# Local attention in front of two dense layers: 12 attention units of two 128-query blocks instead of 16 of two 96-query blocks

## The chip, the cores and the metric

The kernel runs on one core of a Trainium2 chip. The metric is the device time of one execution in microseconds (us); lower is better. Engines are named as in the profile: PE (matmuls), PEld (PE's weight loads), DVE (VectorE), ACT (ScalarE), POOL (GpSimd), and SP, whose queue issues most of the DMAs. Every engine works through its own queue in order.

## The reference

```python
# q, k, v: (4, 8, 768, 64); mem_k, mem_v: (4, 8, 8, 64); chunk, left, right = 32, 16, 8
for c in range(24):                                  # 24 chunks of 32 queries
    q_c = q[:, :, 32*c : 32*c + 32]
    lo, hi = max(0, 32*c - 16), min(768, 32*c + 40)
    k_full = concatenate([mem_k, k[:, :, lo:hi]], axis=2)      # up to 64 keys
    v_full = concatenate([mem_v, v[:, :, lo:hi]], axis=2)
    s = (q_c @ k_full.T) / 8
    a = exp(s - max(s)); a = a / (sum(a) + 1e-9)
    out[:, :, 32*c : 32*c + 32] = a @ v_full
x = out as (3072, 512)
h = (x @ w1) * (x @ w2) @ w3;  x = h @ w_out         # 512 -> 1024 -> 512
y = (x @ w_a) * (x @ w_b) @ w_out2                   # 512 -> 1536 -> 512
```

All data are float32.

## The kernel before

The 3072 tokens are cut into six tiles of 512. A first stretch makes the product of `w3` and `w_out` on PE (tiles `wps`, 32 fp32 matmuls for each of two halves, every one of them two records in the trace). Its weights come as 64-bit words: ACT scales them in two passes (`w_scale`), and DVE joins them in two instructions (`w_bits`). Then, for four of the tiles, come the first dense layer's products (`psA`, `psB`, 12 matmuls each, then `psY`). Last come the seven-product forms of the other tiles and of the second layer (lines 1047 and 1346), which the change does not touch.

Attention is woven into the first stretch and into the four tiles. It goes in units `u`. A unit is two blocks of `GQ` = 96 queries of all 8 heads, 192 tokens, so there are 16 units; the first three lie in the `wps` stretch. Its steps, by their functions:

- `a_k`, `a_q`, `a_v` load raw keys (`kraw`), queries (`q`) and values (`v`) through SP. `a_keys` copies the keys into windows `kw`, on DVE or ACT.
- `a_scores` makes scores `sc`: small matmuls of 64 rows by 32 columns, for 8 head pairs, `NC` = 3 chunks and 2 row halves. A chunk's scores go to 32 partitions of their own, so 2 x 3 places of the PE array are in use. With two records each these are 96 records.
- `a_max` (mask, row maximum, two subtractions into `tt`, on DVE), `a_exp` (two exponentials on ACT) and `a_norm` (sum, reciprocal, two multiplications on DVE) are the softmax.
- `a_trans` transposes `tt` on PE into `pt` (8 transposes); `a_pt` copies that to `p2` on ACT. `a_pv` multiplies it with `v` into `xp`: matmuls of 64 rows by 64 columns in 2 x 2 places, 96 records. `a_x` takes `xp` out as a high part (ACT) and a low part (DVE) `xt`, which `psA` and `psB` read.

Where each step stands in the program is a table. Slot `BASE[u] + s` holds a step; `attn_slot` writes the next slot's steps at fixed places of the `wps` loops (from place `g` = 9 of the first half on, two places to a `k`), and later `between` does so after each `psA` or `psB` (12 matmuls). Buffers are single for `kw`, `q`, `v`, `p2`; there are two `tt`, used in turn.

Of the kernel before, what the change touches and what calls it, by code (L numbers as in the profile page):

```python
# [17 lines left out]
GQ = 96  # L18
NG = S // GQ
KW = 128  # L20
# [27 lines left out]
def tile_attention_moe(  # L48
# [54 lines left out]
    tt = [att.tile([GQ, NH * KR + 1], F32, tag="t", bufs=2, name="tt") for _ in range(2)]  # L103
# [14 lines left out]
    def a_k(u):  # L118
        if u >= NA:
            return  # L120
        k = ks[u] = att.tile([P, NE, 4 * KW], F32, tag="kraw", bufs=1, name="kraw")
# [3 lines left out]
        src = bass.AP(src.tensor, src.offset, [[row[0], P], [step, NE], x])  # L125
        nc.sync.dma_start(out=k, in_=src)

# [26 lines left out]
    def a_keys(u):  # L154
        if u >= NA:
            return
        k = ks.pop(u).rearrange("p e (h k) -> p (e h) k", h=4)
        p, a, e = k.ap
        win = bass.AP(
            k.tensor, k.offset + NMEM * e[0], [p, a, [CHUNK * e[0], NC], [e[0], KEYS - NMEM]]  # L160
        )
        if u in (1, 2):
            nc.scalar.activation(kw[:, :, :, NMEM:], win, AF.Copy)
        else:
            nc.vector.tensor_copy(kw[:, :, :, NMEM:], win)
        if new_batch(u):
            nc.vector.tensor_copy(
                kw[:, :, :, 0:NMEM], k[:, :, None, 0:NMEM].to_broadcast([P, NH, NC, NMEM])
            )

# [20 lines left out]
    def with_eps(u):  # L191
        t = tt[u % 2]
        p, x = t.ap
        return bass.AP(t.tensor, t.offset, [p, [KR * x[0], NH], [(KEYS + 1) * x[0], 2], [x[0], KEYS + 1]])
# [3 lines left out]
    def a_max(u):  # L198
        sc = scs.pop(u)
        for e in range(NE):  # L200
            g = (NE * u + e) % NG
            hs = slice(4 * e, 4 * e + 4)
            if g == 0:
                a_edge(sc, slice(0, CHUNK), hs, NMEM, NMEM + LEFT)
            if g == NG - 1:
                a_edge(sc, slice(GQ - CHUNK, GQ), hs, KEYS - RIGHT, KEYS)
        t = tt[u % 2][:, : NH * KR].rearrange("p (a x) -> p a x", x=KR)[:, :, 1:]
        t = t.rearrange("p a (r k) -> p a r k", r=2)
        mx = att.tile([GQ, 2, NH], F32, tag="mx", bufs=2, name="mx")
# [12 lines left out]
        soft[u] = (sc, t, mx, sm)  # L222
# [87 lines left out]
    for u in range(NA):  # L310
# [22 lines left out]
    at(0, (lambda u: w_load(), 0, False), (a_v, 0, False))  # L333
    NEED = []
    for i in range(NT1):
        u = -(-TT * (i + 1) // (NE * GQ)) - 1
        NEED.append(BASE[u] + (13 if u > 2 else 10))
# [323 lines left out]
    for i in range(2):  # L661
# [14 lines left out]
    whole = []  # L676
# [31 lines left out]
    for half in range(2):  # L708
        banks = [psd.tile([P, 512], F32, tag="d", name="wps") for _ in range(4)]
        for k in range(8):  # L710
            for m in range(4):
# [6 lines left out]
                if half == 0:  # L718
                    if g == 9:
                        amid[:] = [w_turn, w_next]  # L720
                    if g >= 9:
                        attn_slot()
                    if g in (0, 2, 4, 6, 8):
                        w_tick(g < 8)
                    if g == 0:
                        a_k(0)
                        a_q(0)
                    if g == 7:
                        a_keys(0)
                        a_k(1)  # L730
                    if g == 9:
                        bound[0] = len(wsrc)
                    if g == 13:
                        w_turn()
                else:
                    attn_slot()
                    for i in range(2 * len(S3)):
                        if (2, 6, 3, 7, 7, 8, 11, 12)[i] == g:
# [3 lines left out]
                    if g == 9:  # L742
                        split_hi(wsm[0][:, 0, :], whole[0])
                        split_lo(wsm[0][:, 1, :], whole[0], wsm[0][:, 0, :])
                    if g in (1, 4, 5, 6, 9, 10, 13, 14):
                        w_tick()
# [87 lines left out]
    PACE = 6  # L834

    def between():
# [9 lines left out]
        if not converting:  # L846
            for _ in range(1 + (n % PACE == 0)):
# [831 lines left out]
```

## Time and profile before

| | before |
|---|---|
| median of 3 runs | 1030.5 us (1030.47 to 1031.82) |
| the profiled execution's own time | 1030.02 us |
| its span (first to last instruction) | 1028.2 us |
| mean granted TensorE clock | 0.999 |
| PE busy | 1019.4 us (99%) |
| DVE, ACT, POOL busy | 729.0, 493.7, 160.0 us |

The span is what the trace covers; the execution's own time is 1.8 us longer. A busy PE means that some matmul was under way. Matmuls overlap, so a group's summed time and its mean say less than the starts of the groups in the timeline.

### The profile page before, as it was taken

The numbers are of one execution on the slowest core, as the hardware profiler recorded it, in microseconds if no ns is written. First come the engines' busy times: TensorE is split into PE (matmuls) and PEld (weight loads), VectorE is DVE, ScalarE is ACT, GpSimd is POOL, SyncE is SP. The second block draws the span as 40 slices with busy tenths as digits, with TensorE's granted clock in tenths as the row PEclk, the third lists the DMA queues.
The fourth block names the chain that finished last, engine by engine and source line by source line (L and its number), as shares of the span: only waits on it lengthen the run. The fifth ranks groups of instructions, "written<-read, shape, count | busy, mean of one in ns | idle before, by whom it ended". The sixth has DMA issues, their size and how long they took to land.

```text
span 1028.2 us, 18741 instructions
## 1 busy us (share of the span) xinstructions
PE 1019.4 (99%) x7294; PEld 817.0 (79%) x7294; DVE 729.0 (71%) x1158; ACT 493.7 (48%) x886; POOL 160.0 (16%) x210
## 2 busy tenths in 40 slices
PE   9999999999999999999999999999999999999997
PEld 3468888888888888888888888888888888888886
DVE  4879936666565365768777778976677896666695
ACT  5676613444443345565645345643433663344352
POOL 0011397132231100001011101002100000101000
PEclk9999999999999999999999999999999999999999
DMA  8986557778886534496657774987545697324166
GB/s 326 324 225 206 156 200 246 237 231 272 258 296 199 159 115 159 138 317 191 199 188 227 234 251 139 343 235 195 130 156 176 216 310 180 101 87 134 37 205 122
DMA packets 150297, 208.76 MB, mean 203 GB/s; under 512 B 60481, under 2 KB 107457, under 8 KB 148929
## 3 DMA queue, kind: packets, MB, share of 16 engines
q1 hardware_dynamic: 132112, 163.22, 49.5%
q0 software_dynamic: 11008, 42.47, 13.7%
q10 hardware_dynamic: 7088, 1.88, 1.0%
q8 instruction: 57, 0.93, 0.4%
q14 instruction: 32, 0.25, 0.1%
HBM read 157.20 MB, written 52.43 MB: 204 GB/s over the span
## 4 chain that ended last, share of the span: by engine, by line
PE 52%; DVE 1%; issue 0%
PE ps L1047 34%; PE ops L1346 17%; PE psY L97 2%; DVE tmp L1063 0%; DVE g L1073 0%; DVE w L110 0%; DVE ob L1383 0%; DVE tmp L1382 0%; DVE cs L613 0%
## 5 line engine op out<-in xcount | busy, mean ns | idle before, releaser
L1047 PE MATMUL ps<-x,w 128*128 128x512 f32 x1848 | 422.9, 389 | 0.3 <-DVE tmp L1063 0.2
L1047 PEld LDWEIGHTS ps<-x,w 128*128 128x128 f32 x1848 | 346.5, 188 | 73.5 <-DVE tmp L1063 1.4
L1059 ACT ACTIVATE tmp<-ps 128x512 f32<-128x512 f32 x132 | 78.8, 597 | 245.7 <-PE ps L1047 175.8
L1346 PE MATMUL ops<-wo,fo 128*128 128x512 f32 x756 | 174.6, 389 | 0.0
L1346 PEld LDWEIGHTS ops<-wo,fo 128*128 128x128 f32 x756 | 141.8, 188 | 29.9 <-ACT x L1401 0.6
L97 PE MATMUL psY<-g,wo 128*128 128x512 f32 x576 | 134.5, 391 | 0.0
L110 DVE TENSOR_TENSOR w<-w 128x512 fp32r<-128x512 f32 (+1 forms) x176 | 105.5, 619 | 37.7 <-ACT w L107 37.7
L97 PEld LDWEIGHTS psY<-g,wo 128*128 128x128 f32 x576 | 107.4, 188 | 22.4
L1296 DVE TENSOR_TENSOR tmp<-ps,tmp 128x512 f32<-128x512 f32 x108 | 74.3, 688 | 31.9 <-PE ps L1047 27.0
L97 PE MATMUL psA<-xt,w 128*128 128x512 f32 x384 | 94.3, 394 | 0.0
L97 PE MATMUL psB<-xt,w 128*128 128x512 f32 x384 | 93.8, 393 | 0.0
L107 ACT ACTIVATE w<-w 128x512 fp32r<-128x512 f32 (+1 forms) x176 | 92.5, 572 | 0.0
L97 PEld LDWEIGHTS psB<-xt,w 128*128 128x128 f32 x384 | 71.2, 188 | 15.0
L97 PEld LDWEIGHTS psA<-xt,w 128*128 128x128 f32 x384 | 70.9, 188 | 14.9
L1236 DVE TENSOR_TENSOR wo<-gl,wo 128x512 fp32r<-128x512 f32 x90 | 59.6, 685 | 31.6 <-ACT wo L107 31.6
L941 POOL DMA_DIRECT2D w<-wc x36 | 19.4, 540 | 306.9 <-PE ps L1047 275.7
L419 ACT ACTIVATE raw<-raw 128x512 f32<-128x512 f32 (+1 forms) x62 | 46.1, 744 | 32.7 <-DMA raw<-in_wab 18.7
L107 ACT ACTIVATE wo<-gl 128x512 fp32r<-128x512 f32 x90 | 52.9, 625 | 9.3 <-PE ops L1346 8.9
L97 PE MATMUL wps<-w_f 128*128 128x512 f32 x112 | 50.0, 598 | 0.6 <-DVE w_f L425 0.6
L420 ACT ACTIVATE raw<-raw 128x512 uint32<-128x512 uint32 (+1 forms) x62 | 46.1, 744 | 0.0
L780 DVE TENSOR_TENSOR gv<-psB,gv 128x512 f32<-128x512 f32 x32 | 22.0, 686 | 27.1 <-PE psB L97 25.2
L97 PEld LDWEIGHTS wps<-w_f 128*128 128x128 f32 x112 | 20.7, 190 | 25.3 <-issue 21.9
(106 smaller groups left out, 1012.3 us busy)
## 6 DMA issues: line engine op xcount, KB each, us to landing
fo<-fo SPq DMA_DIRECT2D x42, 768.0 KB
w<-wc POOLq DMA_DIRECT2D x36, 512.0 KB, 3.8
w<-wc POOLq DMA_DIRECT2D x36, 384.0 KB, 3.4
raw<-in_wab SPq DMA_DIRECT2D x24, 512.0 KB
v<-in_vw SPq DMA_DIRECT2D x64, 168.0 KB
kraw<-in_kt SPq DMA_DIRECT2D x16, 512.0 KB
raw<-in_w3a SPq DMA_DIRECT2D x6, 1024.0 KB
q<-in_qt SPq DMA_DIRECT2D x16, 384.0 KB
```

Source lines behind the costliest of these rows:

```text
L97: nc.tensor.matmul(o, lhsT=l, rhs=r, start=first, stop=last)
L107: nc.scalar.activation(hi, src, AF.Copy)
L110: nc.vector.tensor_tensor(lo, src, hi.bitcast(F32), ALU.subtract)
L419: nc.scalar.activation(h, h, AF.Prelu, scale=2.0**-112, alpha=2.0**32)
L420: nc.scalar.activation(l, l, AF.Copy, scale=2.0**-29)
L780: nc.vector.tensor_tensor(gv, psB[:, :TT], gv, ALU.mult)
L941: nc.gpsimd.dma_start(out=t[:, 1, :c].bitcast(F32), in_=wseq[n][:, :c])
L1047: nc.tensor.matmul(ps, lhsT=w[i][:, a, k, :], rhs=xs[i][:, b, k, :], start=first and n == 0, stop=n == 5, skip_group_check=not first,)
L1059: nc.scalar.activation(z, ps, AF.Copy)
L1236: low.tensor_tensor(e[:, 1, :n], src, e[:, 0, :n].bitcast(F32), ALU.subtract)
L1296: nc.vector.tensor_tensor(z, ps, y, ALU.add)
L1346: nc.tensor.matmul(ps[s], lhsT=w[:, b, P * s : P * s + P], rhs=e[:, a, :], start=fresh and j == 0 and n == 0, stop=j == HF - 1 and n == 2, ...
```

## The change

A unit is now two blocks of 128 queries, 256 tokens, so there are 12 units, two of them in the `wps` stretch. `NC` is 4: scores use 2 x 4 places of the PE array and 128 partitions. There is one `tt` instead of two. From unit 2 on the raw keys come one block at a time through one buffer `khalf`, and each block's copy into `kw` stands in a slot of its own; a unit then has two key loads and two copies. The first load of attention data comes later, the slots are new, and so are the places where weights are converted in the `wps` stretch. Three of the four first-half results now go out as plain copies (`whole`) and are split into high and low parts later. The weight sums of the later layers (`cw_step`, `d_weights`) start after step 18.

```diff
-GQ = 96
+GQ = 128
-KW = 128
+KW = 160
-    tt = [att.tile([GQ, NH * KR + 1], F32, tag="t", bufs=2, name="tt") for _ in range(2)]
+    tt = [att.tile([GQ, NH * KR + 1], F32, tag="t", bufs=1, name="tt")]
-    def a_k(u):
+    def a_k(u, es=(0, 1)):
...
+        if len(es) == 2:
+            k = p0.tile([P, NE, 4 * KW], F32, tag="kraw", bufs=1, name="kraw")
+            src = bass.AP(src.tensor, src.offset, [[row[0], P], [step, NE], x])
+        else:
+            k = att.tile([P, 1, 4 * KW], F32, tag="khalf", bufs=1, name="khalf")
+            src = bass.AP(src.tensor, src.offset + step * es[0], [[row[0], P], [step, 1], x])
         nc.sync.dma_start(out=k, in_=src)
-    def a_keys(u):
+    def a_keys(u, es=(0, 1)):
...
+        for e in es:
...
+            w = kw[:, 4 * e : 4 * e + 4]
+            if u in (0, 1, 2):
+                nc.scalar.activation(w[:, :, :, NMEM:], win, AF.Copy)
+            else:
+                nc.vector.tensor_copy(w[:, :, :, NMEM:], win)
-    BASE = [0, 6, 13, 23, 29, 36]
-    NX = len(BASE)
-    BASE += [BASE[-1] + 7 * i for i in range(1, NA - NX + 1)]
-    SLOTS = {0: (6, 7, 9, 10), 1: (6, 7, 10, 11), 2: (6, 7, 8, 8)}
+    BASE = [5, 12]
+    BASE += [25, 33, 41, 48, 56, 64, 71, 79, 86, 94]
+    SLOTS = {0: (6, 8, 8, 10), 1: (6, 6, 9, 9)}
-        if u > 0:
-            at(BASE[u] - 3, (a_keys, u, True))
-            at(BASE[u] - 2, (a_k, u + 1, True))
+        if u == 1:
+            at(BASE[0] + 0, (a_k, 1, False))
+            at(BASE[1] - 3, (a_keys, 1, True))
+        if u > 1:
+            at(BASE[u] - 7, (a_half(a_k, 0), u, False))
+            at(BASE[u] - 6, (a_half(a_keys, 0), u, True))
+            at(BASE[u] - 6, (a_half(a_k, 1), u, True))
+            at(BASE[u] - 3, (a_half(a_keys, 1), u, True))
-        if half == 0 and m == 0:
-            whole.append(stage.tile([P, 4, CH // 2], F32, tag="cs", bufs=2, name="whole").rearrange("p i c -> p (i c)")[:, :CH])
-            nc.scalar.activation(whole[0], banks[m], AF.Copy)
+        if half == 0 and m < 3:
+            if m % 2 == 0:
+                keep[:] = [stage.tile([P, 4, CH // 2], F32, tag="cs", bufs=2, name="whole").rearrange("p i c -> p (i c)")]
+            whole.append(keep[0][:, CH * (m % 2) : CH * (m % 2) + CH])
+            nc.scalar.activation(whole[m], banks[m], AF.Copy)
             return
-        if not converting:
-            for _ in range(1 + (n % PACE == 0)):
+        if not converting and n > 18:
+            for _ in range(1 + (n % 6 == 0)):
```

What the program's order becomes shows at three places. First PE, from the program's start, before: `wps` is the product of `w3` and `w_out`, `sc`, `pt` and `xp` are a unit's scores, transposes and values; the count behind an x is of matmuls.

```order
L97 MATMUL wps<-w_f 128x512 x20
L97 MATMUL sc<-kw,q 32x64 x48
L97 MATMUL wps<-w_f 128x512 x12
L249 MATMUL pt<-id_sb,tt 128x96 x8
L97 MATMUL sc<-kw,q 32x64 x48
L97 MATMUL wps<-w_f 128x512 x6
L97 MATMUL xp<-p_400,v 64x32 x48
```

And PE at the same place now:

```order
L97 MATMUL wps<-w_f 128x512 x30
L97 MATMUL sc<-kw,q 32x64 x64
L97 MATMUL wps<-w_f 128x512 x12
L260 MATMUL pt<-id_sb,tt 128x128 x8
L97 MATMUL wps<-w_f 128x512 x2
L97 MATMUL sc<-kw,q 32x64 x64
L97 MATMUL wps<-w_f 128x512 x2
L97 MATMUL xp<-p_476,v 64x32 x64
```

Unit 0's scores moved from behind the 20th `wps` matmul to behind the 30th, two before the end of the first half (32 matmuls), and a unit has 64 small matmuls where it had 48.

Second ACT, around the end of the first `wps` half, before (`raw` are weights being scaled, `whole` and `wo` take the first half's four results out of PE's banks):

```order
L419 ACTIVATE raw_208<-raw_208 128x1024
L420 ACTIVATE raw_208<-raw_208 128x1024
L227 ACTIVATE tt<-tt 96x4x128 x2
L163 ACTIVATE kw<-kraw 128x24x56
L682 ACTIVATE whole<-wps 128x512
L684 ACTIVATE wo<-wps 128x512 x3
L255 ACTIVATE p_400<-pt 128x768
```

ACT at the same place now:

```order
L434 ACTIVATE raw_208<-raw_208 128x1024
L435 ACTIVATE raw_208<-raw_208 128x1024
L434 ACTIVATE raw_217<-raw_217 128x1024
L435 ACTIVATE raw_217<-raw_217 128x1024
L699 ACTIVATE whole<-wps 128x512
L238 ACTIVATE tt<-tt 128x4x128 x2
L699 ACTIVATE whole<-wps 128x512 x2
L701 ACTIVATE wo<-wps 128x512
```

One more weight block is scaled ahead of the first result, and unit 0's two exponentials now stand between the first result's copy and the second's.

Third DVE in the tiles, now, around one unit's softmax: `kw<-khalf` is the copy of one block of the next unit's keys, and `gv<-psB` takes PE's `psB` results.

```order
L200 TENSOR_TENSOR sc<-sc,mask_sb 32x2x4x16
L222 TENSOR_REDUCE mx<-sc 128x16
L227 TENSOR_TENSOR tt<-sc,mx 128x2x4x64 x2
L793 TENSOR_TENSOR gv<-psB,gv 128x512
L246 TENSOR_REDUCE sm<-tt 128x16
L247 RECIPROCAL sm<-sm 128x16
L249 TENSOR_TENSOR tt<-tt,sm 128x4x128
L173 COPY kw<-khalf 128x16x56
L796 TENSOR_TENSOR g_2126<-gv,g_2126 128x512
L249 TENSOR_TENSOR tt<-tt,sm 128x4x128
L793 TENSOR_TENSOR gv<-psB,gv 128x512
```

The copy of a block's keys moved into the middle of the unit before, one slot behind the load that it needs, and a `gv<-psB` stands behind it on DVE.

## Rows read from the trace of the kernel before

**Rows 1.** The page, part 1: busy us, share of the span, instructions.
```profile
PE 1019.4 (99%) x7294; PEld 817.0 (79%) x7294; DVE 729.0 (71%) x1158; ACT 493.7 (48%) x886; POOL 160.0 (16%) x210
```

**Rows 2.** Busy us by stretch, with granted clock, DMA share and GB/s.
```profile
core 0: us, PE busy (x) PEld busy (x) DVE busy (x) ACT busy (x) POOL busy (x), PEclk, DMA share, GB/s
26.00:76.00 50.00, 48.64 (x698) 27.27 (x697) 39.27 (x55) 36.28 (x51) 5.12 (x4) 1.00 0.87 275
30.00:35.00 5.00, 5.00 (x13) 2.24 (x12) 4.80 (x7) 3.41 (x4) 0.00 (x0) 1.00 1.03 401
...
76.00:360.00 284.00, 284.00 (x3635) 233.08 (x3634) 182.11 (x269) 127.46 (x219) 100.85 (x106) 1.00 0.70 224
```

**Rows 3.** PE's waits over the span: total us, times, longest us.
```profile
PE wps L97 <- DVE w_f L425: 0.6, 2, 0.3
PE pt L249 <- issue: 0.6, 1, 0.6
...
PE sc L97 <- DVE kw L167: 0.2, 1, 0.2
```

**Rows 4.** PE's timeline, one unit's period in the tiles: start us, us.
```profile
237.71 1.19 PE L97 MATMUL sc<-kw,q 64*32 64x64 f32 x96
238.84 3.02 PE L97 MATMUL psB<-xt,w 128*128 128x512 f32 x12
241.69 0.82 PE L249 MATMUL pt<-id_sb,tt 96*128 96x96 f32 x8
...
247.95 1.60 PE L97 MATMUL xp<-p,v 64*64 64x32 f32 x96
...
252.34 2.88 PE L97 MATMUL psB<-xt,w 128*128 128x512 f32 x12
255.06 2.88 PE L97 MATMUL psA<-xt,w 128*128 128x512 f32 x12
257.87 1.19 PE L97 MATMUL sc<-kw,q 64*32 64x64 f32 x96
```

**Rows 5.** PE's groups by form: busy us, mean ns of one.
```profile
L97 PE MATMUL xp<-p,v 64*64 64x32 f32 x1536 | 25.7, 220 | 0.0
L97 PE MATMUL sc<-kw,q 64*32 64x64 f32 x1536 | 19.1, 219 | 0.2 <-DVE kw L167 0.2
L249 PE MATMUL pt<-id_sb,tt 96*128 96x96 f32 x128 | 13.5, 247 | 0.6 <-issue 0.6
```

**Rows 6.** PE's timeline at the start of the first stretch.
```profile
9.23 17.33 PE L97 MATMUL wps<-w_f 128*128 128x512 f32 x40
```

**Rows 7.** Timeline of the first stretch: a weight block, unit 0's softmax, the results.
```profile
25.78 0.33 SPq L404 DMA_DIRECT2D raw<-in_w3b  x1
...
30.65 0.29 DVE L189 TENSOR_TENSOR sc<-sc,mask_sb 32x128 f32<-32x128 f32 x1
...
30.97 1.22 DVE L211 TENSOR_REDUCE mx<-sc 96x16 f32<-96x1024 f32 x1
...
33.40 1.17 ACT L419 ACTIVATE raw<-raw 128x1024 f32<-128x1024 f32 x1 [1.59 <-DMA raw<-in_w3b]
...
34.06 1.28 DVE L216 TENSOR_TENSOR tt<-sc,mx 96x512 f32<-96x512 f32 x2
...
34.46 1.13 ACT L420 ACTIVATE raw<-raw 128x1024 uint32<-128x1024 uint32 x1
...
35.48 1.15 ACT L227 ACTIVATE tt<-tt 96x512 f32<-96x512 f32 x2
...
38.21 1.56 ACT L684 ACTIVATE wo<-wps 128x512 fp32r<-128x512 f32 x3
```

**Rows 8.** Timeline at the end of the first stretch.
```profile
73.13 1.60 PE L97 MATMUL xp<-p,v 64*64 64x32 f32 x96
...
74.82 0.87 ACT L107 ACTIVATE xt<-xp 128x512 fp32r<-128x512 f32 x2 [1.37 <-PE xp L97]
...
76.16 2.88 PE L97 MATMUL psA<-xt,w 128*128 128x512 f32 x12
```

More of the change, by code (lines that the diff above doesn't have):

```diff
@@ L124, in a_k @@
         step = 2 * 2 * D * row[0]
-        src = bass.AP(src.tensor, src.offset, [[row[0], P], [step, NE], x])
+        if len(es) == 2:
[4 more added lines that the diff above has]
+            src = bass.AP(src.tensor, src.offset + step * es[0], [[row[0], P], [step, 1], x])
         nc.sync.dma_start(out=k, in_=src)
+        for e in es:
+            ks[u, e] = k[:, e if len(es) == 2 else 0]
     def a_q(u):
@@ L152, in a_v, with a_half @@
                 nc.sync.dma_start(out=v[D * r + NMEM : D * r + D, e, :, :], in_=win)
-    def a_keys(u):
+    def a_keys(u, es=(0, 1)):
         if u >= NA:
             return
[L157 to L168, printed above, removed]
-            )
+        for e in es:
+            k = ks.pop((u, e)).rearrange("p (h k) -> p h k", h=4)
+            p, a, x = k.ap
+            win = bass.AP(
+                k.tensor, k.offset + NMEM * x[0], [p, a, [CHUNK * x[0], NC], [x[0], KEYS - NMEM]]
+            )
+            w = kw[:, 4 * e : 4 * e + 4]
[3 more added lines that the diff above has]
+                nc.vector.tensor_copy(w[:, :, :, NMEM:], win)
+            if new_batch(u):
+                nc.vector.tensor_copy(
+                    w[:, :, :, 0:NMEM], k[:, :, None, 0:NMEM].to_broadcast([P, 4, NC, NMEM])
+                )
+    def a_half(f, e):
+        return lambda u: f(u, (e,))
     def a_scores(u):
@@ L191, in with_eps @@
     def with_eps(u):
-        t = tt[u % 2]
+        t = tt[0]
         p, x = t.ap
@@ L206, in a_max @@
                 a_edge(sc, slice(GQ - CHUNK, GQ), hs, KEYS - RIGHT, KEYS)
-        t = tt[u % 2][:, : NH * KR].rearrange("p (a x) -> p a x", x=KR)[:, :, 1:]
+        t = tt[0][:, : NH * KR].rearrange("p (a x) -> p a x", x=KR)[:, :, 1:]
         t = t.rearrange("p a (r k) -> p a r k", r=2)
-        mx = att.tile([GQ, 2, NH], F32, tag="mx", bufs=2, name="mx")
+        mx = att.tile([GQ, 2, NH], F32, tag="mx", bufs=1, name="mx")
         sm = att.tile([GQ, NH, 2], F32, tag="sm", bufs=2, name="sm")
@@ L336, in tile_attention_moe @@
         u = -(-TT * (i + 1) // (NE * GQ)) - 1
-        NEED.append(BASE[u] + (13 if u > 2 else 10))
+        NEED.append(23 if i == 0 else BASE[u] + 13)
     acount = [0]
@@ L660, in tile_attention_moe @@
     nc.vector.memset(wz, 0.0)
-    for i in range(2):
+    for i in range(1):
         p, x = tt[i].ap
@@ L718, in tile_attention_moe @@
                 if half == 0:
-                    if g == 9:
-                        amid[:] = [w_turn, w_next]
                     if g >= 9:
                         attn_slot()
-                    if g in (0, 2, 4, 6, 8):
-                        w_tick(g < 8)
-                    if g == 0:
+                    if g in (0, 2, 4, 7, 8, 10, 12):
+                        w_tick(g < 99)
+                    if g == 6:
                         a_k(0)
                         a_q(0)
+                    if g == 8:
+                        a_keys(0)
                     if g == 7:
-                        a_keys(0)
-                        a_k(1)
-                    if g == 9:
                         bound[0] = len(wsrc)
-                    if g == 13:
-                        w_turn()
                 else:
@@ L737, in tile_attention_moe @@
                     for i in range(2 * len(S3)):
-                        if (2, 6, 3, 7, 7, 8, 11, 12)[i] == g:
+                        if (6, 8, 9, 11)[i] == g:
                             w_split(i)
@@ L741, in tile_attention_moe @@
                         w_next()
[L742 to L745, printed above, removed]
+                    for m1, g1 in enumerate((7, 8, 10)):
+                        if g == g1:
+                            split_hi(wsm[m1][:, 0, :], whole[m1])
+                            split_lo(wsm[m1][:, 1, :], whole[m1], wsm[m1][:, 0, :])
+                    if g in (0, 1, 4, 5, 9, 11, 13, 15):
                         w_tick()
@@ L832, in tile_attention_moe @@
     NA1 = NB * (ND - 1) + 2 * M1 - 4
-    PACE = 6
     def between():
```

5 lines of the change are left out of this document (2 added, 3 removed).

## The prediction

> **What bounds the kernel now.** The busy shares come first: PE is busy for 99% of the span, DVE for 71% [rows 1]. The table by stretch says where the missing per cent lies: from 76 to 360 us, where 13 of the 16 units run beside the tiles, PE is busy for 284.00 of 284.00 us; in the first stretch it lacks 1.36 of 50 us [rows 2]. PE's own waits name that stretch's idle time: 0.6 us for weights from DVE, 0.6 us ahead of a transpose, 0.2 us for keys, 1.4 us in all [rows 3]. So PE's queue sets the time everywhere. What DVE and ACT save with fewer and longer softmax instructions is hidden under PE: in the tiles DVE is busy for 182 of 284 us [rows 2], and nothing waits for it. The change can move the time in two ways only: by what attention's small matmuls cost PE, and by new waits of PE.
>
> **What a unit costs PE.** A busy PE says nothing of cost, since matmuls overlap; the starts in the timeline do [rows 4]. From one unit's scores (237.71) to the next unit's (257.87) are 20.16 us. In between stand six groups of 12 large matmuls (`psB` and `psA` in turn, three shown), and an undisturbed one takes 255.06 - 252.34 = 2.72 us. 20.16 - 6 x 2.72 = 3.84 us is what one unit's scores, transposes and values cost, with their run-in and run-out. Sixteen units cost 61.4 us.
>
> Now each part for 128 queries. The counts of matmuls and of columns over all units are the same (16 x 48 = 12 x 64 small ones, 128 x 96 = 96 x 128 transposed columns), so only what a unit pays once, and how well its matmuls overlap, can change.
>
> Values: 96 records take 1.60 us less the last one's 0.22, so 14.4 ns each [rows 4, 5]. The 2 x 2 places stay, so 32 more records cost 32 x 14.4 = 0.46 us.
>
> Transposes: 8 in 0.82 us, less the last one's 0.25, are 81 ns for 96 columns [rows 4, 5]. 128 columns take 109, so 8 cost 0.22 us more.
>
> Scores are the unknown: 96 records on 2 x 3 places start within 1.19 - 0.22 = 0.97 us, 10.1 ns each [rows 4, 5]. Two things could set this. If it is the place, then a record keeps its place as long as its columns last: 40 records of 512 columns took 17.33 us [rows 6], 0.846 ns a column, 54 ns for 64 columns. 16 records for each of six places make 0.87 us, nearly all of 0.97. With 2 x 4 places it is still 16 records for each, and 64 matmuls cost no more than 48 did: 0 more. If it is the handing out of records, 32 more cost 32 x 10.1 = 0.32 us. I take the middle, 0.16: the place explains most of the 0.97, but eight records within each 54 ns is denser than anything that these rows show.
>
> A unit then costs 3.84 + 0.46 + 0.22 + 0.16 = 4.68 us, and twelve 56.2: **5.2 us saved**. The ends are 7.2 us (12 x 4.52) and 3.3 us (12 x 4.84, rounded).
>
> [...] No row here shows eight places at work.
>
> **New waits in the first stretch.** PE starts `wps` at 9.23 and takes 0.433 us a record [rows 6]; with no scores inside, the 60 records ahead of unit 0's scores end at 35.2. Weights can follow: the keys and queries that stood ahead of the last two weight blocks now stand behind them on SP's queue. The scores end at about 36.4, the half's last two matmuls at 38.2. The second half then wants the four banks of the first.
>
> ACT takes them out, and its order is new. Ahead of the first result it now scales two blocks. The first arrived at 33.4 [rows 7]; its transfer now has 0.26 MB more ahead of it, unit 0's larger key and query blocks (128 partitions x 2 x 128 words more of each), 0.65 us at 401 GB/s [rows 2]. Each block takes 1.17 + 1.13 us [rows 7], so ACT is free at 38.6 and the first bank at 39.2: PE waits 1.0 us. Next on ACT are the exponentials, which wait for DVE's mask, maximum and subtractions: 36.4 + 0.29 + 1.22 + 1.28 = 39.2 [rows 7], so they are ready to run, 1.15 us [rows 7], and only then comes the second bank, 1.15 + 0.5 us after the first (three results take 1.56 [rows 7]). PE's first matmul of the second half lasts 0.87 us, so it waits another 0.8 to 0.9. Together **1.9 us**; an early weight block only moves the wait from the first bank to the second, since the exponentials hold the second until about 40.9 anyway. The other two results follow at the pace at which PE needs them.
>
> Behind that wait DVE has the third weight block's joining behind the softmax again, the kind of wait that cost 0.3 us each before [rows 3]: 0.3. At the stretch's end the high part of `xt` comes out of unit 1's values. Before, ACT took it 0.09 us after PE was done (73.13 + 1.60 to 74.82), because ACT was idle, and PE had 1.4 us of other matmuls left [rows 8]. Now a key copy, a weight block and one result stand ahead of it on ACT, and it is 1024 elements long where it was 768. Between no wait and 1.1 us I take the middle, 0.5. That makes 2.7 us of waits. The 1.4 us of before go, as each of its places is gone or moved: **1.3 us lost**, between -0.5 and 3 us as the transfers fall.
>
> **Steps costed at nothing.** One `tt`: DVE's subtraction waits until PE has transposed the unit before, which stands one slot or less ahead, 2.72 us; behind it on DVE is a `psB` result, which PE has not made by then either. The key copies in halves: 20 loads and 24 copies in place of 16 and 16, on queues that PE doesn't wait for as long as a copy is less late than the `psB` behind it can be; four banks give that three groups, 8.2 us. If that cover goes, see the third rival. The weight sums that start after step 18 lie on POOL, busy for 101 of 284 us [rows 2]; they are read only in the last of the four tiles.
>
> **The sum.** 1030.02 (this execution) - 5.2 + 1.3 = 1026.1 us. The median of the three runs stands 0.5 us above this execution, so **1026.6 us**. A measurement of this kernel can tell about 0.2%, 2.1 us, from no change: faster means below 1028.4, slower above 1032.6.
>
> **Rivals.**
>
> *The scores are bound by handing out.* Then 3.3 us are saved, and with 1.3 us of waits the time is 1028.5: no change that can be told. For it speaks that 0.97 is a tenth more than the places need; against it that six places explain the rest.
>
> *The scores are bound by the place alone.* 7.2 us saved: 1030.5 - 7.2 + 1.3 = 1024.6.
>
> *Late keys: slower.* The first block's load is written one slot ahead of its copy, behind the `q` load on SP, which itself waits for the scores; the second load waits for the first copy, in one buffer. The copies stand on DVE ahead of a `gv<-psB`. If a load landed more than 2.7 + 8.2 = 10.9 us after its issue, PE would run out of banks, once in each of ten units. Against it: the weight block that arrived at 33.4 had been issued at 25.8 [rows 7], 7.6 us before, with other large transfers ahead of it and the queues full at DMA share 1.03, where the tiles have 0.70 [rows 2]. At 12 us, PE would lose 10 x 1.1 us and the time be 1037.6; from 11.5 us on (0.6 x 10 against 3.9, and 2.1 more) it is slower. [...] No row here shows a key load alone.
>
> *A unit costs the same per query.* If run-in and run-out grew with the unit, or a fourth place for 32 partitions drained PE each time, nothing would be saved and the waits would stay: 1031.8. Against it stand the starts of the rows, which give 2 x 2 and 2 x 3 places a steady pace of 14.4 and 10.1 ns.
>
> **How the numbers follow.** Forecast (half-way scores) 0.40, place alone 0.20, handing out 0.20, same per query 0.09, late keys 0.11. The first two are below 1028.4: faster 0.60; the next two within the bound: 0.29; slower 0.11. The range goes from 1023.5 (place alone with a us less of waits than taken) to 1030.8 (handing out and waits near 3 us, with 0.5 to spare); late keys and the last rival, 0.20, lie outside above.
>
> **What would show it.** A period of the tiles with a unit in it, less its 2.72 us groups: 4.68 us if right, 4.52 or 4.84 at the ends. The scores' group, 128 records: 1.19 to 1.51 us long. In the first stretch two waits of about a us at the start of the second `wps` half, on ACT's results, and the first `psA` at about 75. PE idle between 76 and 360 us would prove the steps costed at nothing wrong, and an idle PE behind `gv` or `kw` the third rival right. The forecast fails if PE's new waits in the first stretch pass 3.5 us, which a late block of weights or keys would do, since SP, ACT and DVE have been re-ordered there together.

## The result, and the profile after

The changed kernel takes 1037.4 us (median of 14 runs, 1031.5 to 1042.3), the kernel before 1030.7 on the same chip (14 runs, 1029.1 to 1032.6): ratio 1.0056, interval 1.0038 to 1.0074. It is slower, by 0.56% as that ratio has it and by 6.7 us as the medians have it, where 1026.6 was forecast; not even its fastest run reaches that. Two things are to be explained: a median 11 us too high, and runs that now differ by 11 us where those of before differ by 3.5. The profiled execution took 1034.39 us with the clock granted in full almost throughout (mean 0.999; span 1032.6), so it shows less than the typical loss.

First the views that answer to [rows 1 to 4]. The page's line of the engines, and one of its DMA queues (packets, MB, share), which the argument needs later:

```profile
PE 1017.4 (99%) x7262; PEld 816.6 (79%) x7262; DVE 713.3 (69%) x1133; ACT 491.5 (48%) x872; POOL 157.0 (15%) x209
...
q8 instruction: 57, 0.93, 0.4%
```

The stretches of [rows 2] again:

```profile
core 0: us, PE busy (x) PEld busy (x) DVE busy (x) ACT busy (x) POOL busy (x), PEclk, DMA share, GB/s
26.00:76.00 50.00, 45.35 (x574) 24.13 (x574) 33.45 (x45) 35.32 (x50) 5.58 (x4) 1.00 0.81 256
76.00:360.00 284.00, 281.11 (x3721) 232.46 (x3714) 171.79 (x253) 123.88 (x204) 97.74 (x106) 1.00 0.74 222
```

The first stretch, which lacked 1.36 us, lacks 4.65; and the tiles, in which PE was never idle, lack 2.89 of 284 us. By the prediction's own words that proves something "costed at nothing" wrong. PE's waits over the span say what (against 1.4 us in [rows 3]):

```profile
PE sc L97 <- issue: 2.0, 1, 2.0
PE psA L97 <- issue: 1.6, 1, 1.6
...
PE wps L97 <- ACT whole L699: 1.3, 2, 1.0
PE sc L97 <- ACT kw L171: 0.7, 1, 0.7
PE psA L97 <- DVE w L470: 0.6, 1, 0.6
PE psB L97 <- DVE w L470: 0.4, 1, 0.4
PE xp L97 <- issue: 0.3, 1, 0.3
PE psA L97 <- ACT w L476: 0.2, 1, 0.2
PE wps L97 <- DVE w_f L440: 0.2, 1, 0.2
```

Three kinds stand here. The first bank waits and the weights of `w_f`, 1.5 us, are those that were forecast (1.9 and 0.3). Unit 1's keys (0.7) and, in the tiles from 100 to 108 us, the `w` of w12 (1.2) were not. But the most, 3.9 us, are three waits for **issue**: PE waits for nothing that the profile shows. A reader must not stop at that word.

What a unit costs, by the starts as in [rows 4]:

```profile
236.46 2.88 PE L97 MATMUL psA<-xt,w 128*128 128x512 f32 x12
239.28 1.48 PE L97 MATMUL sc<-kw,q 64*32 64x64 f32 x128
240.69 3.03 PE L97 MATMUL psB<-xt,w 128*128 128x512 f32 x12
243.56 1.03 PE L260 MATMUL pt<-id_sb,tt 128*128 128x128 f32 x8
244.35 3.01 PE L97 MATMUL psA<-xt,w 128*128 128x512 f32 x12
247.20 2.88 PE L97 MATMUL psB<-xt,w 128*128 128x512 f32 x12
249.92 2.88 PE L97 MATMUL psA<-xt,w 128*128 128x512 f32 x12
252.73 2.07 PE L97 MATMUL xp<-p,v 64*64 64x32 f32 x128
254.73 3.02 PE L97 MATMUL psB<-xt,w 128*128 128x512 f32 x12
257.58 1.75 PE L97 MATMUL psA<-xt,w 128*128 128x512 f32 x7
```

An undisturbed group lasts 249.92 - 247.20 = 2.72 us as before. Scores 240.69 - 239.28 = 1.41, transposes 0.79, values 2.00, and what the five groups beside them last over 2.72 (2.82, 2.87, 2.85, 2.81, 2.85) is 0.60: 4.80 us. Forecast were 4.68, with 4.84 as the handing-out end.

### The profile page after: what moved, and what is told of

It reads as the page before. It is cut to its first block, busy times and chain, and to the rows that moved or that the text cites. A ratio compares the mean times of both kernels' runs of the same rounds, so it can differ in the third digit from the quotient of the medians.

```text
span 1032.6 us, 18569 instructions
## 1 busy us (share of the span) xinstructions
PE 1017.4 (99%) x7262; PEld 816.6 (79%) x7262; DVE 713.3 (69%) x1133; ACT 491.5 (48%) x872; POOL 157.0 (15%) x209
## 4 chain that ended last, share of the span: by engine, by line
PE 52%; DVE 1%; ACT 0%; issue 0%
PE ps L1058 33%; PE ops L1357 17%; PE psY L97 2%; DVE tmp L1074 0%; DVE g L1084 0%; DVE w L110 0%; DVE ob L1394 0%; DVE tmp L1393 0%; DVE cs L628 0%; ACT tmp L1070 0%
## 5 line engine op out<-in xcount | busy, mean ns | idle before, releaser
L439 DVE TENSOR_SCALAR dec<-raw 128x512 uint32<-128x512 uint32 x48 | 22.8, 474 | 33.9 <-ACT raw L434 33.9
```

What stands on the lines that cost most here:

```text
L439: nc.vector.tensor_scalar(a, h, 3, None, ALU.logical_shift_left)
```

## The experiments

Each time stands against the kernel before, run beside it (medians 1030.2 to 1031.2). Theory W: the loss is the waits for banks, keys and weights. Theory B: PE's queue of instructions runs dry where small matmuls stand together.

**The changed kernel again** (no edit).

> The changed kernel unaltered, to see what one more profile of it shows beside the first. The first profiled execution took 1034.4 us, 3 us less than the median of the changed kernel's runs (1037.4, from 1031.5 to 1042.3), with a clock granted in full almost everywhere. Theory W (new waits in the first stretch, the same each time): a second profile has the same waits of PE at the same places within 0.3 us, and the 3 us stay unexplained by them. Theory B (PE's queue runs dry for some us where it gets 272 small matmuls at a stretch, nothing named as the releaser, sooner or later as the transfers fall): the idle times without a releaser lie at other places and have other lengths than in the first profile (there 2.2 us inside unit 1's scores, 0.5 inside unit 0's values, 1.8 behind a unit at 319), and where one is long the granted clock falls to half for some us after it. Median expected by both: 1037, ratio 1.006.

1037.5 us (1032.7 to 1042.1), ratio 1.0067 [1.0043, 1.0090]. PE's timeline between unit 1's scores and unit 0's values, first of the first profile, then of this one:

```profile
49.84 1.88 PE L97 MATMUL wps<-w_f 128*128 128x512 f32 x4
52.46 1.58 PE L97 MATMUL sc<-kw,q 64*32 64x64 f32 x115 [0.73 <-ACT kw L171]
56.05 0.34 PE L97 MATMUL sc<-kw,q 64*32 64x64 f32 x13 [2.01 <-issue]
56.32 1.98 PE L97 MATMUL wps<-w_f 128*128 128x512 f32 x4
58.23 1.82 PE L97 MATMUL xp<-p,v 64*64 64x32 f32 x109
60.38 0.54 PE L97 MATMUL xp<-p,v 64*64 64x32 f32 x19 [0.33 <-issue]
```

```profile
54.01 1.83 PE L97 MATMUL sc<-kw,q 64*32 64x64 f32 x128 [2.71 <-ACT kw L171]
55.77 3.48 PE L97 MATMUL wps<-w_f 128*128 128x512 f32 x4
59.18 1.82 PE L97 MATMUL xp<-p,v 64*64 64x32 f32 x109
62.99 0.54 PE L97 MATMUL xp<-p,v 64*64 64x32 f32 x19 [1.99 <-issue]
```

The reader is to see the counts. Unit 0's values break off after the 109th of 128 in both profiles, once for 0.33 us, once for 1.99. Unit 1's scores break after the 115th in the first; in the second, where they had waited 2.7 us for keys, they don't. A wait for data has a tile as its releaser; this one has none, stands at a fixed place in the queue, inside a group, and has another length each time. Behind the second wait-ridden stretch (3.3 us without a start) four large matmuls took 3.48 us in place of 1.88: the clock was granted at half for 3.4 us (55.4 to 58.8). The third such place is the 1.6 us in the tiles:

```profile
316.09 1.03 PE L260 MATMUL pt<-id_sb,tt 128*128 128x128 f32 x8
317.05 1.48 PE L97 MATMUL sc<-kw,q 64*32 64x64 f32 x128
318.46 1.19 PE L97 MATMUL psA<-xt,w 128*128 128x512 f32 x4
321.29 2.01 PE L97 MATMUL psA<-xt,w 128*128 128x512 f32 x8 [1.63 <-issue]
```

Here 136 small matmuls of the page follow one another, and PE stands behind the fourth large one. To find the place in PE's queue, count all its instructions: for each matmul of the page a weight load and a multiplication, and also the semaphore and drain instructions that the trace has on PE and the page leaves out (83 in all; 6, 10 and 36 ahead of the three places). Counted so, the pair at which PE stood begins with its 705th, 961st and 7873rd instruction: 193 + 2 x 256, + 3 x 256, + 30 x 256 (the pair's weight load is recorded before the wait, at 53.79, 59.81 and 319.27 us, its multiplication after it, so an edge is placed to within one instruction). PE's 14,607 instructions (2 x 7262 + 83) divided by the 57 packets of queue q8, kind "instruction", are 256, and 0.93 MB in 57 packets are 16.3 KB each. So PE's instructions come in blocks of 256, and PE stood at edges of blocks (that q8 is PE's is read from this count and from the times below). The other runs bear it out: the 16 profiles of the changed kernel and its variants name 20 waits for issue, all 20 stand at such an edge, and each ends 1.1 to 1.7 us after a packet of q8 has landed. (The 0.6 us of issue in the kernel before, ahead of a transpose, are at no edge.)

When does a block come? The packets by queue from 48.5 us, when PE passes the edge at instruction 449, to 53.4, and from there to 56.0:

```profile
DMA packets 886, 0.94 MB, mean 191 GB/s; under 512 B 72, under 2 KB 823, under 8 KB 885
...
q1 hardware_dynamic: 885, 0.93, 99.0%
q14 instruction: 1, 0.01, 0.8%
DMA packets 268, 0.27 MB, mean 106 GB/s; under 512 B 22, under 2 KB 266, under 8 KB 266
...
q1 hardware_dynamic: 266, 0.25, 45.7%
q8 instruction: 1, 0.02, 3.2%
```

From 48.5 to 53.4 us the data queue q1 (the rest of unit 1's keys, then v's loads) had all engines busy, and no packet of q8 moved; it came at 53.4, landed at 54.7, and PE went on at 56.05, in the block that begins at instruction 705, as counted here. **In this stretch a block's fetch started late: 1.5 to 5.3 us after PE had passed the edge before it.** That the data transfers hold the fetch up is a reading of these times and not shown. Against it stands that a packet of q14, another queue of kind "instruction", came through amid the data (50.7 to 51.3 us), and that in the second profile, where PE passed the edge at 55.35, no packet of any queue moved from 55.7 to 56.9, and the fetch still began only at 60.65, behind unit 2's queries and w12's loads that set in at 56.9:

```profile
DMA packets 0, 0.00 MB, mean 0 GB/s; under 512 B 0, under 2 KB 0, under 8 KB 0
```

Before the change fetches started as late (4.1 us behind the edge at 27.2), but the shortest time between two edges in the first 100 us was 6.3 us (edges at 74.4 and 80.7), since its runs of 96 or 104 small matmuls, 192 or 208 instructions, always leave 24 large ones in a block. A run of 128 fills a block whole.

**Unit 0's exponentials one slot later.**
```diff
-            (int(u > 0), a_max),
+            (1, a_max),
...
-            (int(u > 0), a_exp(0)),
-            (int(u > 0), a_exp(1)),
+            (1, a_exp(0)),
+            (1, a_exp(1)),
```

> Unit 0's maximum and exponentials are written one slot later, so that ACT takes three results of the first half before the exponentials. Theory W: the wait of 1.2 us at the second bank of the second half goes (0.2 left), and if nothing else waits for the exponentials the time falls by 1.0 us, to 1036.4 by the median (ratio to the kernel before 1.0047). Theory B: the place of the exponentials has nothing to do with PE's queue; the wait goes, but the idle times without a releaser, 4 us in the first profile, stay, and the spread of the runs with them.

1036.5 us, ratio 1.0069 [1.0045, 1.0093]. The second bank's wait fell from 1.0 us (1.4 in the second profile) to 0.4, and nothing was gained: in the profile 2.4, 1.5 and 1.3 us of issue waits stand at the same three edges, and 1.8 us for keys.

**Unit 1's key load two slots earlier.**
```diff
-            at(BASE[0] + 0, (a_k, 1, False))
+            at(3, (a_k, 1, False))
```

> Unit 1's key load is written two slots earlier, ahead of the last weight block and of the w12 loads on SP's queue. Theory W: the wait for the key copy ahead of unit 1's scores (0.9 us at 51.1 us) goes and the time falls by about 1 us, less what the later weight block gives back (0.33 MB at 400 GB/s are 0.8 us, for one matmul of the half): 1036.4 to 1037.2. Theory B: the 0.9 us go too, but unit 1's scores then start earlier and the idle time without a releaser inside them (2.2 us) moves with them or changes its length as the transfers beside it do; median between 1035 and 1038.

1032.9 us (1029.6 to 1037.3), ratio 1.0024 [1.0010, 1.0038]: 4.6 us less, from a wait of 0.7 to 2.7. Before, the load was issued at 40.80, behind w12's and unit 1's queries on SP, and the copy could start at 51.45; now it was issued at 30.49. The keys' wait went, and with it the one inside unit 0's values, since that block's fetch now started at 55.5 us and landed at 56.6, ahead of its edge at 57.9. The 1.7 us inside unit 1's scores, after the 115th, stayed. Neither theory had so much.

**Scores in two halves in the tiles.**
```diff
+    def a_scores(u, part=0):
...
+        for a in range(4 * part, 4 * part + 4):
...
+            (int(u > 1), lambda u: a_scores(u, 1)),
+            (int(u > 1), lambda u: a_q(u + 1)),
```

> The scores of units 2 to 11 in two halves of 32 matmuls, one slot apart; nothing in the first stretch changes. Theory W (and the unit costs read from the starts): a half more has one more run-in and run-out of about 0.2 to 0.4 us, so 10 units lose 2 to 4 us and the median is 1039 to 1041. Theory B: PE gets at most 144 small matmuls at a stretch in the tiles, so the idle times without a releaser in the tiles (1.8 us at 319 in the first profile, others in other runs) go: median 1034 to 1037, and the runs spread over 4 us in place of 11.

1037.2 us, ratio 1.0076 [1.0054, 1.0097]. The wait at instruction 7873 is gone, as B says; ten more run-ins cost about 0.3 us each, as W says (from the first `psA` to the first `ps` 313.1 us with 0.3 of waits, where the first profile took 312.8 with 2.8); the spread stayed, for it is born in the first stretch, where this profile has the longest wait of all at the same 109th of the values:

```profile
PE xp L97 <- issue: 4.0, 1, 4.0
```

So the time alone decides nothing here; the next runs move the edges and nothing else.

**The edges moved: 200, 52 and 72 instructions more ahead of the first weight product.** Only the warm-up multiplications change, in time in which PE waits for weights; each call is four instructions. The diff of 72 (for 200 it has 3 and 52 calls in place of 4 and 19; 52 more are 4 and 14, of 40 columns each where no mend goes with them):
```diff
-    for _ in range(5):
+    for _ in range(4):
         mm(warm[:GQ], wz[:, :GQ], wz, True, True)
+    for i in range(19):
+        c = CHUNK * (i % NC)
+        mm(warm[c : c + CHUNK, :D], wz[:D, :CHUNK], wz[:D, :D], True, True)
```

> The changed kernel with 200 instructions more on PE ahead of the first weight product (one wide and 54 narrow warm-up multiplications in place of five wide ones), in time in which PE waits for the first weights anyway; nothing else is changed. Theory B, now sharper: PE's instructions come in blocks of 256; the fetch of a block starts when PE enters the block before it, and takes 2.5 to 7.6 us until PE can go on. In four profiles of the changed kernel and its variants PE stood at records 705, 961 and 7873 of its queue, that is 193 + 256 n, whatever was there. With 200 more the edges lie at 251, 507, 763 and so on as counted with the new ones: the one at 319 us (edge right behind 136 small matmuls) goes, unit 0's values and unit 1's scores still lie within one block (4 us), so one wait of 1 to 3 us there stays in place of two. Time by B: 2 to 4 us less than the changed kernel, 1033.5 to 1035.5 by the median (ratio to the kernel before 1.003 to 1.005). Theory W (the waits are those for banks, keys and values): the extra warm-up changes nothing, 1037 (ratio 1.0065).

That run missed its aim: 54 narrow multiplications (128 x 40) took so long that the first weight product started at 26.2 us, some 17 late, and the time was 1046.9, ratio 1.0153 [1.0136, 1.0169]; its profile has no wait for issue. It was done again with short ones:

> Again the changed kernel with 200 instructions more ahead of the first weight product, now as three wide and 52 small warm-up multiplications (32 x 64, on places in turn), since the narrow ones took about 0.2 us each and held up the first weight product by 17 us (26.2 instead of 8.5 to 8.9), in which the transfers got ahead. Counted from the first weight product that run took 1012.3 us, against 1017.9 and 1018.1 in the two profiles of the changed kernel and 1012.9 of the kernel before. Theory B: the edge at 319 us is gone here too, and in the first stretch one unnamed wait of 1 to 3 us is left, where unit 0's values follow unit 1's scores within one block (edges 705 to 961 as counted here): 1034 to 1036. If the head start of the transfers was what helped there, the first stretch stays at 70 to 72 us from the first weight product to the first tile, and the time is 1035 to 1037.

**1031.6 us (1030.0 to 1033.1), ratio 1.0001 [0.9992, 1.0010]: 5.8 us less, and a spread of 3 us, with the work and its order untouched.** The timeline of the same place:

```profile
34.87 1.48 PE L97 MATMUL sc<-kw,q 64*32 64x64 f32 x128
...
40.79 8.31 PE L97 MATMUL wps<-w_f 128*128 128x512 f32 x18 [1.28 <-ACT whole L702]
...
51.62 1.48 PE L97 MATMUL sc<-kw,q 64*32 64x64 f32 x128
...
55.15 2.47 PE L97 MATMUL xp<-p,v 64*64 64x32 f32 x128
```

No group breaks any more (unit 0's values last 2.47 us where 2.07 is usual); only the forecast bank wait stands there (40.79). One edge in the tiles still costs 0.7 us, at 326 us inside another unit's values.

> The same with 52 instructions more (four wide and 14 narrow warm-up multiplications in place of five wide ones). Theory B: the edges at 141 and 397 now take in all of unit 0's 128 scores, so PE must stand 2 to 3 us near record 397 (in the last few scores of unit 0 or just behind them, at 36 us), where the changed kernel has no wait; there is one edge within unit 1's scores (record 653) and one within unit 0's values (909), with 1 to 3 us of wait; in the tiles one of 1 to 2 us near 217 us (1.6 us for a block) in place of the one at 319. Median 1038 to 1041, ratio 1.007 to 1.010. Theory W: 1037 as before, and no wait in or behind unit 0's scores.

1032.3 us, ratio 1.0013 [1.0000, 1.0026]: less by 5, where more was expected. The new edge was where it should be, behind the 127th of unit 0's scores, but cost 0.5 us only, and the two others fell where the queues were free: theory B had the places right and the delay of a fetch too long for them.

> The changed kernel with nothing but 72 instructions more of warm-up, the third place for the edges with the work the same (0 more: 1037.4; 200 more: 1031.6). Theory B: no wait at an edge in the first stretch but at most 1 us within unit 0's values; what stays are unit 1's keys (1 to 2 us), the banks (1.5 us) and w12 (1 us): 1031 to 1032.5, ratio 1.000 to 1.002. If 200 more helped by something else than the edges (an earlier granted clock, a longer warm-up), 72 more help less than half as much: 1034 to 1036.

1033.0 us, ratio 1.0013 [1.0001, 1.0026]. No issue wait in the profile; the waits for banks (2.3 us) and `w_f` (1.5) have grown, and the clock was at half for 3.4 us behind them (from 43.4). And the control, 52 more in the kernel before:

> The kernel before with 52 instructions more of warm-up. Theory B: its runs of small matmuls have 96 to 104, 192 to 208 instructions, so that each block of 256 takes in at least 24 large matmuls wherever its edge lies (6.3 us was the shortest in its profile, the next block was there at the least 3 us sooner): no shift can make it wait. Ratio 1.000 within 0.002. If it moves by more than 0.2%, the warm-up itself (clock, first weights) has an effect, by which the two runs above have to be corrected.

1030.7 us, ratio 0.9997 [0.9987, 1.0007]: nothing.

**What is left with the waits mended too.** Unit 1's key load earlier ("key") and unit 0's exponentials later ("exp"), under the shifts; first a run with the key load, the values of unit 0 three slots later and the long warm-up.

> Three edits together: unit 1's key load two slots earlier, unit 0's values three slots later (6 large matmuls, 2.6 us), and 200 instructions more of warm-up. Theory B: no block of 256 instructions in the first stretch is used up in less than 5.5 us, so PE's unnamed waits there go but for half a us, and the one at 319 too; what stays are the waits for banks (1.6 us) and for w12 (1 us). 1033 less 3 to 4 us: 1029 to 1030, ratio 0.998 to 1.000, and the runs spread over 4 us. Theory W: 1033, as with the key load alone, or more, because unit 1's values now follow unit 0's sooner (v has one buffer).

1049.5 us, ratio 1.0174 [1.0157, 1.0190]; of it some 17 us are again the late start, and 2.4 us a wait of the first `psA` for `xt`, which now lies behind other work on ACT. Like the other run with the late start its profile has no wait for issue, so of spreading the values it shows the new wait and no gain.

> Unit 1's key load two slots earlier, and 52 instructions more of warm-up (14 small ones). In the run with 52 more the edges lay at 36.8 and 55.0 us, so that no block was entered between 40 and 54 us, where a fetch takes longest (4.4 to 5.3 us to its start, in the profiles of the changed kernel); what it still waited for was unit 1's keys, 1.8 us, which go here. Theory B: 1031 us, below both the key load alone (1032.9) and the shift alone (1032.3). If the gains are the same gain twice, 1032 to 1033.

1029.4 us, ratio 0.9980 [0.9969, 0.9990].

> The same with unit 0's maximum and exponentials one slot later, which shortened the wait at the banks of the second half from 1.6 to 0.6 us when tried alone, while the time stayed the same because waits behind it grew. If those are gone now, 1 us less than without it: 1030, ratio 0.999 to 1.000; if PE waits for something else in that stretch instead, no difference.

1028.4 us (1026.8 to 1032.3), ratio 0.9975 [0.9964, 0.9987]: **faster than both kernels**, than the one before by a quarter of a per cent, with a wait at the edge in unit 0's scores still in it. That wait in the profile with 52 and the key load:

```profile
34.99 1.47 PE L97 MATMUL sc<-kw,q 64*32 64x64 f32 x127
38.43 0.24 PE L97 MATMUL sc<-kw,q 64*32 64x64 f32 x1 [1.97 <-issue]
```

> Unit 1's key load two slots earlier, unit 0's exponentials one slot later, and 72 instructions more of warm-up (19 small multiplications). With 52 more, one block held all of unit 0's scores and PE stood 2.2 to 2.6 us at their end (36 to 38 us), once with the granted clock down for 6.8 us behind it. With 72 more the block that ends within unit 0's scores begins 10 large matmuls ahead of them, 5.4 us in place of 2.2, so by theory B that wait goes, and no other edge is nearer than 3.7 us at a time of full transfers. 1028.4 less 1.5 to 2.5 us: 1026 to 1027, ratio 0.995 to 0.997. If the wait moves behind it instead (keys, banks), 1028 to 1029.

1031.6 us, ratio 0.9997 [0.9981, 1.0012]. The wait at that edge is gone, and the gain isn't there: PE comes earlier to data that isn't there yet.

```profile
PE xp L97 <- DMA v<-in_vw: 0.9, 2, 0.5
...
PE sc L97 <- DMA q<-in_qt: 0.5, 1, 0.5
```

> Both mends (unit 1's key load two slots earlier, unit 0's exponentials one slot later) with 200 instructions more of warm-up, the shift that alone gave 1031.6. If the edges and the two waits are separate losses, the bank wait (1.5 us in that run, 0.6 with the exponentials later) goes by 0.9 and the time is 1030.5 to 1031, ratio 0.999 to 1.000; the earlier scores of unit 1 bring the edge in unit 0's values (960, as counted here) 1 us nearer to the fetch before it, which may take it all back: 1031.6. If the first stretch is bound by the arrival of weights and v whatever PE waits for, 1031 to 1032 too, as with 72 more.

1032.8 us, ratio 1.0013 [1.0002, 1.0024]: a wait of 0.7 us at the edge in unit 0's values, where 200 alone lost 0.4 at most, and 1.9 for w12.

> Both mends without any shift. By the edges alone: the key load earlier gave 1032.9, with one wait of 2 us at the edge in unit 1's scores; the exponentials later take away 1 us at the banks, and bring that edge as much nearer to its late fetch: between 1032 and 1033 (ratio 1.001 to 1.003), so that 52 more on top of both mends (1028.4) are worth 3.5 to 4.5 us. If the shift were worth nothing, it would be 1028.4 here too.

1032.2 us, ratio 1.0018 [1.0002, 1.0034]: 1.9 us at the edge in unit 1's scores are back, and 1.1 for unit 1's queries. The medians in one table:

| instructions more | no mend | key | key and exp |
|---|---|---|---|
| 0 | 1037.4 | 1032.9 | 1032.2 |
| 52 | 1032.3 | 1029.4 | 1028.4 |
| 72 | 1033.0 | | 1031.6 |
| 200 | 1031.6 | | 1032.8 |

Without a mend every shift takes off 4.4 to 5.8 us; with both, 52 takes off 3.8, but 72 and 200 nothing that these runs can tell (0.6 less and 0.6 more; the intervals overlap). The edges and the waits for data cover each other.

**The old places of the weight steps**, on top of 52, key and exp:
```diff
-                    if g in (0, 1, 4, 5, 9, 11, 13, 15):
+                    if g in (1, 4, 5, 6, 9, 10, 13, 14):
```

> The same with the steps of the weight conversion in the second half of the first stretch at the places of the kernel before (1, 4, 5, 6, 9, 10, 13, 14 in place of 0, 1, 4, 5, 9, 11, 13, 15). In the tiles from 100 to 108 us the changed kernel waits 1.2 to 1.7 us for w12 weights, which the kernel before does not. If the places of these steps make them late, the waits go and the time falls by another us, to 1029; if the loads behind unit 2's keys on SP's queue do, nothing changes.

1037.1 us, ratio 1.0060 [1.0041, 1.0078]. The w12 waits from 100 to 108 us are gone, but the work that these steps displace is late at the end of the stretch and just behind it (79 to 85 us), for more, and PE that comes later gives w12 time as well:

```profile
PE psB L97 <- DVE wo L705: 2.6, 1, 2.6
PE psA L97 <- ACT xt L107: 1.9, 1, 1.9
```

## Why the prediction was wrong

**The step that failed** is the sentence that the change "can move the time in two ways only: by what attention's small matmuls cost PE, and by new waits of PE", with the new waits sought only where PE waits for data (banks, weights, `xt`). PE must have its instructions too, and their arrival was put at nothing without a reason: waits for them took 3.9 us in the first profile. [Rows 1] hold 7294 matmuls and as many weight loads, and nothing in the rows that were read says how they arrive; the page's queue of kind "instruction" was passed over. The prediction weighed whether 128 small matmuls can be handed to their places fast enough, and not whether they are there. With 96 in a run they were, with the edges in either place (control: 0.9997). With 128 a run can use up a block in 1.4 us, and where PE stood at an edge, it went on 3 to 9 us after it had passed the edge before. By the traces a block is 256 instructions (57 packets of 16.3 KB for 14,607 instructions), and there is one fetch to an edge, which in the first 100 us began between 1.9 us before PE's record at that edge and 4.9 us after it in the first profile. In the kernel before no wait at an edge shows it; in the first profile of the changed kernel three do.

How much of the loss it is: with the edges alone moved, 1037.4 became 1031.6 to 1033.0, so **4.4 to 5.8 of the 6.7 us**. Of the 10.8 us by which the forecast was missed the unit's size, below, is 1.4 more; the other 3.6 to 5.0 are not divided among the keys, w12's weights and what else differs from run to run. In the edges' share lies what can follow an edge: in some executions the clock was at half behind a stand of PE, for 3.4 us in the second profile (behind 3.3 us without a start, which were a wait for keys) and for 6.8 us in the one below; behind the edge wait of 2.0 us in the first profile it stayed at 1.00. In the profile with 52, key and exp, which at 1031.6 us is one of the slowest of its runs, a 2.4 us edge wait ends at 39.95, and in 6.8 us PE gets through 8 matmuls:

```profile
core 0: us, PE busy (x) PEld busy (x) DVE busy (x) ACT busy (x) POOL busy (x), PEclk, DMA share, GB/s
39.50:46.30 6.80, 6.35 (x8) 2.64 (x9) 4.46 (x6) 4.61 (x8) 0.00 (x0) 0.50 1.03 384
```

The spread of the runs fits: in the six profiles without a shift the same edge costs 0 to 2.0 us in unit 1's scores and 0 to 4.0 in unit 0's values. The longest profiled execution without a shift has 1041.4 us (scores in two: edge waits of 4.4 us, and 10.2 us at half the clock); that the longest of the others are this and nothing else is only argued.

**The unit** was mis-sized: 4.80 us measured for 4.68. Values +0.47 (0.46 forecast) and transposes +0.18 (0.22) held; the scores took 0.28 more for 0.16, near the end called "bound by handing out" (0.32). Eight places gave hardly anything over six: 128 records started within 1.48 - 0.23 = 1.25 us, 9.8 ns each, where 96 took 10.1. 61.4 - 12 x 4.80 = 3.8 us saved, not 5.2.

**The waits of the first stretch** came out right in sum in one run, and not term by term. From the first weight product to the first `psA` the kernel before took 76.16 - 9.23 = 66.9 us. Less its waits (1.4) and the unit that has moved (3 x 3.84 - 2 x 4.80 = 1.9) these are 63.6, plus the 2.7 forecast 66.3; with hardly an edge in the way it took 74.98 - 8.61 = 66.4 (200 more) but 79.07 - 8.97 = 70.1 (72 more, with longer bank waits and the half clock). In the first profile of the changed kernel it took 78.28 - 8.49 = 69.8, in the second 80.87 - 8.90 = 72.0. The two banks cost 1.3 us together where 1.9 were told, and `xt` (0.5 forecast) cost nothing, so that 66.4 agrees with 66.3 is in part luck; unit 1's keys, 0.7 to 2.7, were not in the sum at all: their load stood behind w12's and behind unit 1's queries on SP's queue, and landed 10.6 us after its issue.

**Costed at nothing**: the one `tt`, the halved key loads and copies held, as no wait of PE in the tiles names `tt`, `khalf` or `kw` (DVE waited 3.5 us for two of the key loads, and PE did not feel it). That PE would not be idle there did not: an edge cost 1.6 us at 321, and w12's weights come late, 1.2 us at 100 to 108. Whether the new order of the weight steps makes them so isn't settled; the old order, tried with the mends, is worse (1037.1).

**The rivals.** "Bound by handing out" was nearly right about the scores and would have given 1028.5; that the best mended version stands there is chance, as its waits are others. "Late keys" had the sign and a transfer as its cause, but not in the tiles, and its time of 1037.6 agrees with the measured one by luck, for another reason. "The same per query" is refuted by 4.80 us for 128, where 3.84 for 96 would make 5.12.

What stays open: the profiled execution lost 4.4 us against that of before. The issue waits (3.9) and the other waits (3.4), less the 1.4 of before, 3.8 saved and a first weight product 0.7 earlier, give +1.4; each of some nine gaps costs about 0.2 more between starts than it is idle (53.82 to 56.05 are 2.2 for 2.01 idle), which makes 3.2. The last 1.2 us were not traced. Nor was it tried to load v at another time, which would show directly whether its transfers hold up the fetch at 48.5 us; why a fetch starts late stays open.

## What to carry to other kernels

Count the instructions of a run of short matmuls against the block in which PE's instructions come (256 here: 14,607 instructions with weight loads and semaphore instructions, 57 packets). Here runs of 96 (192 instructions) had no wait at an edge and runs of 128 (256 instructions in 1.4 us) up to 4.0 us; moving the edges took 4.4 to 5.8 us off the time, and halving the runs in the tiles took away the wait there, at about 0.3 us for each further run-in. A wait with no releaser whose place in the queue is the same modulo 256 wherever it appears was the sign of it (20 of 20 in 16 profiles), and a few useless instructions at the start, in time that PE waits anyway, told here that edges were a cause. Causes that cover each other do not add: mend one, and look at the next profile before the other.

## What the runs showed of the hardware that was not expected

Each edge has one fetch: 57 packets for 57 edges in both profiles of the changed kernel. From passing an edge to the start of the fetch it was 0.9 us with the queues nearly idle (52 and key: edge at 54.5 us, fetch at 55.4; the stretch is below, DMA share 0.04) and 4.4 to 5.3 us at the three edges between 48 and 56 us that PE passed without standing in the two profiles of the changed kernel, with v's or w12's transfers ahead of the fetch. Where large matmuls stand, the fetch started up to 4.8 us before the record at its edge (435.9 us against 440.7 in the first profile); that PE's queue takes instructions in ahead of their start is a reading of this and not shown. The fetch itself took 0.9 to 1.7 us in the first 100 us, and from its landing to a waiting PE's next record it was 1.1 to 1.7 us.

```profile
core 0: us, PE busy (x) PEld busy (x) DVE busy (x) ACT busy (x) POOL busy (x), PEclk, DMA share, GB/s
54.50:56.00 1.50, 1.50 (x68) 0.98 (x57) 0.80 (x1) 0.00 (x0) 0.00 (x0) 1.00 0.04 11
```

Narrow warm-up multiplications on the whole array were slow: 108 records of 40 columns held the first weight product up to 26.2 us, 0.21 us each, where small ones of 64 columns on places in turn left its start at 8.6. Half of that fits a clock that was still low: the first weight products behind them started 0.85 us apart up to 28.9 us and 0.43 from 29.5 on, and in the run with 52 more, where the clock was full from 4.6 us, records of 40 columns took 0.11 us. The first profile has the same two paces: its warm-up records of 512 columns start 0.85 us apart up to 6.74 us and 0.43 from 7.20 on, and its record of a full clock begins at 6.8.
